# A spectral filter and a PReLU feed-forward block: the first transform's array in another order, its tail in halves, and its first filter load in two parts

## The chip, the cores and the metric

The kernel runs on one core of a Trainium2 chip. The metric is the device time of one execution in microseconds (us). The engines are PE (TensorE: matrix products, with its own weight loads, written PEld), DVE (VectorE), ACT (ScalarE), POOL (GpSimd, which here mostly issues DMAs that convert from float32 to float16), and SP (SyncE, which issues plain DMAs). They run beside each other, each through its own instructions in order, and wait for each other on semaphores. PE writes its results to PSUM, from which ACT or DVE copies them ("evicts" them) to SBUF.

## The reference

```python
X = np.fft.rfft(x, axis=1)                       # x: 8 x 3008 x 256
Y = X * (filt_r + 1j * filt_i)[None, :, :]       # filters: 1505 x 256
y = np.fft.irfft(Y, n=3008, axis=1)
h = y.reshape(24064, 256) @ w_in                 # 256 x 2048
g = np.maximum(h, 0.0) + alpha * np.minimum(h, 0.0)
out = g @ w_out                                  # 2048 x 256
```

So each of the 8 batches is transformed along its 3008 rows, multiplied by one filter, transformed back, and every row then goes through a feed-forward block of width 2048.

## The kernel before

The length 3008 is split as 94 x 32. A transform is a product with a 94-point table, a turn (a transposition), a product with a 32-point table, the filter, the inverse 32-point product, another turn, and the inverse 94-point product. The feed-forward block works on blocks of 512 (one of 384) rows: `Block.up` multiplies by `w_in`, ACT evicts, DVE makes the PReLU, and `Block.down` multiplies by `w_out`. The program is laid out by hand: the text order is the order on each engine.

Seven of the eight transforms are spread in small steps over the feed-forward work of earlier batches (`plan_fft`, `put`), and their turns go through DRAM. The first transform (class `First`, batch 0) has nothing to hide behind. It runs alone at the start, and its turns are products with the identity on PE. Its stages, with the lines of the profile:

- POOL issues the loads of x for batch 0 (L118, eight DMAs), then the filter. `load_filt` (L132-143) issues, for each of the two parts (real, imaginary) and each e in 0, 1, two DMAs of 16 partitions: eight DMAs a call. The calls are for the frequency groups 0 to 4 (L434), 4 to 8 (L455), and 8 to 12, whose real part (L463) and imaginary part (L465) stand on either side of `swapped(8, nc.gpsimd)` (L464), two small POOL operations that make a second inverse table; `swapped(16, nc.gpsimd)` (L468) follows. At group 4 of the loop over groups, POOL issues the loads of `w_in` (L484), of batch 1's x and of `w_out` (L487); a tiny DVE memset of `win_s` (L482) holds the `w_in` loads back until DVE has come that far. Each POOL DMA uses one of eight semaphores in turn, so an issue waits until the DMA issued eight places earlier has landed.
- `piece_a` (L322-336): the 94-point product, eight pieces. The last two pieces are evicted in two parts each, f=0 by ACT and f=1 by DVE, out of one PSUM tile of two banks.
- `turn_at` (L338-345): the first turn, products of `am` with the identity `id16` (L343).
- `piece_b(kp)` for the groups kp = 0 to 11: the 32-point product (L355) and the filter, one DVE product of 128 x 1024 (L360) that reads the filter's group kp.
- `piece_c(kp)`: the inverse 32-point product (L382). Here the filtered data `u` is the stationary operand, the tables `twi_s` and `twx_s` stream; the result goes to PSUM with d on the partitions. `keep_c` evicts it to `vm`, an array of 6144 columns in the order (g, q, k, e), where 4g + e is the row index s and (q, k) the 96 values that the turn puts on partitions.
- `turn` (L393-400): for each s, the 96 columns of `vm` with that s are loaded as the stationary operand. In the order before, neighbours among them are four elements (8 bytes) apart. 64 such products in all (L399): `half_t` makes two values of s, `piece_t` four.
- `half_d` and `pair_d`: the inverse 94-point product (L283) with the table `wi3_s`, whose rows stand in the order (q, k), and the eviction into `yT`, from which the first block starts (`Block.up4`, L569).

After the last group come a fill of three idle products (`warm(3)`, L506, which keep PE busy), `half_t(0)` and `half_t(1)`, evicted by DVE and ACT, two more `half_t` whose eviction comes later, and `half_d(0)` and `half_d(2)`, the two halves of d of the first 376 rows. `up4` multiplies 256 rows by four column groups of `w_in`, both halves kt of d in turn for each group h.

Of the kernel before, what the change touches and what calls it, by code (L numbers as in the profile page):

```python
# [25 lines left out]
def _build_consts():  # L26

    n1, n2, p = np.arange(N1), np.arange(N2), np.arange(32)
    k1 = (2 * (np.arange(NK) // 2) + 24 * (np.arange(NK) % 2))[None, :] + np.arange(2)[:, None]
    k2 = np.where(p < 16, p, 47 - p)  # L30
    g = np.where(p < 16, 1.0, -1.0)

    a1 = 2 * np.pi * n1[:, None, None] * k1[None] / N1
    wf1 = np.stack([np.cos(a1), -np.sin(a1)], axis=2)
    scale = np.where((k1 == 0) | (k1 == 47), 1.0, 2.0)[None, :, None, :] / NFFT
    wi3 = (wf1 * scale).reshape(N1, 96).T
    wfx = wf1.transpose(0, 3, 1, 2).reshape(N1, 96)
# [10 lines left out]
    return wf1, wfx, wfq, wi3, twf  # L48


@with_exitstack
def kernel(
# [8 lines left out]
    out: bass.AP,  # L61
):
    nc = tc.nc
    names = ("wf1", "wfx", "wfq", "wi3", "twf")
# [22 lines left out]
    wfq_s = konst.tile([128, 64], FP16, name="wfq_s")  # L87
    wfx_s = konst.tile([N1, 96], FP16, name="wfx_s")
    wi3_s = konst.tile([96, N1], FP16, name="wi3_s")
    twf_s = konst.tile([128, NK, 64], FP16, name="twf_s")  # L90
    twi_s = konst.tile([128, NK, 64], FP16, name="twi_s")
    filt_s = konst.tile([128, 12, 2, D], FP16, name="filt_s")
# [36 lines left out]
            nc.gpsimd.dma_start(out=hi[32:47], in_=xrow(b, c)[79:94])  # L129
        return lo, hi  # L130

    def load_filt(eng, dst, ha, hb, parts=(0, 1)):  # L132
        n = hb - ha
        for i in parts:
            src = (filt_r, filt_i)[i]
            for e in range(2):
                q = 64 * e + 32 * i
                k = 2 * ha + 24 * e
                for j, step, off in ((0, 1, k), (16, -1, N1 - k)):
                    eng.dma_start(  # L140
                        out=dst[q + j : q + j + 16, ha:hb].rearrange("p h r d -> p (h r) d"),
                        in_=bass.AP(tensor=src.tensor, offset=src.offset + off * D,
                                    ap=[[N1 * D, 16], [step * D, 2 * n], [1, D]]))
# [15 lines left out]
    class Fft:  # L159
        def __init__(self, b):  # L160
            self.b = b
            self.base = (b % 2) * NFFT
            self.uw = {}

        def start_a(self):
# [114 lines left out]
        def inverse(self, pd, g, dh, mh):  # L280
            ps = pd[:, 0 : 4 * N1].rearrange("p (m x) -> p m x", m=4)
            for m in range(4):
                nc.tensor.matmul(ps[:, m], self.zt[:, 8 * g + 4 * mh + m, dh * 128 : dh * 128 + 128],  # L283
                                 wi3_s, start=True, stop=True)
            return ps

        def half_d(self, i, evict, kind, fill=0):
# [19 lines left out]
    def on_dve(o, i):  # L307
        nc.vector.tensor_copy(o, i)  # L308
# [4 lines left out]
    class First(Fft):  # L313
# [7 lines left out]

        def piece_a(self, i, wide):  # L322
            c, sh = i // 2, i % 2
            ps = banks(wide)
            for f in range(2):
                for u in range(4):
                    o = (4 * sh + u) * D + 128 * f
                    nc.tensor.matmul(ps[:, f, 96 * u : 96 * u + 96], xc[(0, c)][0:N1, o : o + 128], wfx_s,
                                     start=True, stop=True)
            o = self.am.rearrange("p (f m s) -> p f m s", f=2, s=N2)[:, :, :, 4 * i : 4 * i + 4]  # L330
            s = ps[:, :, 0:384].rearrange("p f (s m) -> p f m s", s=4)
            if i < 6:
                both[i % 2](o, s)
            else:
                for f in range(2):
                    both[f](o[:, f], s[:, f])

        def turn_at(self, kp, n, evict, wide=False):  # L338
            ps = banks(wide)
# [7 lines left out]
        def piece_b(self, kp):  # L347
            hp = psH.tile([128, 2, 512], FP32, name="hps").rearrange("p r (i d) -> p r i d", i=2)
            for i in range(2):
                for par in range(2):  # L350
                    r = slice(64 * par, 64 * par + 64)
                    for e in range(2):
                        for c in range(2):
                            o = 64 * e + 32 * c
                            nc.tensor.matmul(hp[o : o + 32, par, i],  # L355
                                             twf_s[r, 2 * kp + e, 32 * i : 32 * i + 32],
                                             self.at[kp // 6][r, 2 * kp + e - 12 * (kp // 6)],
                                             start=True, stop=True)
            uu = p_uw.tile([128, 2, 2, D], FP16, name="uu", bufs=3)
            nc.vector.tensor_mul(uu, hp, filt_s[:, kp].unsqueeze(2).to_broadcast([128, 2, 2, D]))  # L360
            self.uw[kp] = uu

        def piece_c(self, kp):
# [7 lines left out]
                self.ops = [t.rearrange("p (k d) -> p k d", k=2) for t in pf]  # L371
            kb = 0 if kp > 9 else kp % 2
            u = self.uw.pop(kp)
            tw, tx = (t.rearrange("p k (c g e) -> p k g c e", c=2, e=4) for t in (twi_s, twx_s))
            for par in range(2):
                for f in range(2):
                    for i, t in enumerate((tw, tx)):
                        for e in range(2):
                            r = slice(64 * e, 64 * e + 64)
                            o = self.ops[e][:, kb].rearrange("p (g w) -> p g w", g=16)  # L380
                            o = o[:, 8 * f : 8 * f + 8, 8 * par : 8 * par + 8]
                            nc.tensor.matmul(o.rearrange("p g (c e) -> p g c e", c=2),  # L382
                                             u[r, par, i, 128 * f : 128 * f + 128], t[r, 2 * kp + par],
                                             start=(i == 0), stop=(i == 1))

        def keep_c(self, kp, evicts, n=2):
            vm = self.vm.rearrange("p (g q k e) -> p g q k e", q=4, k=NK, e=4)
            for e in range(2):
                k = 2 * kp + e
                evicts[e](vm[:, :, :, k : k + 2 * n - 1 : 2],  # L390
                          self.ops[e][:, 0:n].rearrange("p k (g q e) -> p g q k e", q=4, e=4))

        def turn(self, pt, i, n):  # L393
            m = self.vm.rearrange("p (g m e) -> p g m e", m=96, e=4)
            for u in range(n):
                for f in range(2):
                    o = 256 * (u % 2) + 128 * f
                    s = n * i + u
                    nc.tensor.matmul(pt[0:96, u // 2, o : o + 128], m[:, 8 * f + s // 4, :, s % 4], id16,  # L399
                                     start=True, stop=True)  # L400

        def half_t(self, i, kind):
            pt = bank(kind).unsqueeze(1)
# [22 lines left out]
    def swapped(ka, eng):  # L426
        t, o = twi_s[:, ka : ka + 8], twx_s[:, ka : ka + 8]
        eng.tensor_scalar(o[:, :, 32:64], t[:, :, 0:32], gs_s, None, OP.mult)
        eng.tensor_scalar(o[:, :, 0:32], t[:, :, 32:64], gs_s, -1.0, OP.mult, OP.mult)

    xc = {(0, c): load_x(0, c) for c in range(4)}
    f0 = First()
    table(0, 8)
    load_filt(nc.gpsimd, filt_s, 0, 4)  # L434

    def warm(n, pw):
        for _ in range(n):
# [23 lines left out]
    f0.turn_at(2, 2, on_act)  # L461
    inverse_table(8, bank("o"))
    load_filt(nc.gpsimd, filt_s, 8, 12, (0,))  # L463
    swapped(8, nc.gpsimd)  # L464
    load_filt(nc.gpsimd, filt_s, 8, 12, (1,))  # L465
    f0.piece_b(1)
    inverse_table(16, bank("o"))
    swapped(16, nc.gpsimd)  # L468
    f0.piece_b(2)
    f0.turn_at(4, 2, on_act)  # L470
    nc.sync.dma_start(out=wi3_s, in_=consts["wi3"].ap())
# [4 lines left out]
    for r in (slice(0, 64), slice(64, 128)):  # L476
        nc.sync.dma_start(out=wfq_s[r], in_=consts["wfq"].ap()[r])
    for kp in range(12):
        if 0 < kp < 10:
            f0.piece_b(kp + 2)  # L480
        if kp == 4:
            nc.vector.memset(win_s[:, :, 0:1], 0.0)  # L482
            for kt in range(2):
                nc.gpsimd.dma_start(out=win_s[:, kt], in_=moe_w_in[kt * 128 : (kt + 1) * 128])  # L484
# [19 lines left out]
    for o in (32, 96):  # L504
        nc.gpsimd.dma_start(out=filt_s[o : o + 32], in_=filt_s[o - 32 : o])
    warm(3, bank("h"))  # L506
    on_dve(*f0.half_t(0, "o"))
    on_act(*f0.half_t(1, "o"))
    later = [f0.half_t(2, "h"), f0.half_t(3, "f")]
    f0.half_d(0, on_act, "o")  # L510
    f0.half_d(2, on_dve, "o")

    sizes = [512] * 5 + [384] + [512] * 6
    blocks = []
# [21 lines left out]
    class Block:  # L536
# [227 lines left out]
```

## Time and profile before

| what | value |
|---|---|
| median of three runs | 773.95 us (772.74 to 774.29) |
| the profiled execution, its own time | 772.3 us |
| its span, first to last instruction | 770.5 us |
| PE busy | 760.9 us (99%) |
| DVE busy / ACT busy / POOL busy | 634.2 (82%) / 583.2 (76%) / 147.9 us (19%) |
| granted TensorE clock | 1.00 of full speed |

By stretches of the span (busy time of each engine in us, from the view by windows):

| stretch, us | PE | DVE | ACT | POOL | what runs |
|---|---|---|---|---|---|
| 0 to 16.8 | 14.15 | 5.32 | 5.67 | 12.01 | loads, `piece_a`, first turns |
| 16.8 to 30.7 | 12.68 | 13.78 | 11.06 | 12.53 | the twelve groups |
| 30.7 to 34.2 | 3.08 | 1.48 | 2.12 | 0.51 | last group, turn, inverse |
| 34.2 to 47 | 12.04 | 9.80 | 9.58 | 3.60 | first block, more turns |
| 47 to 72 | 24.85 | 22.39 | 20.16 | 2.05 | feed-forward, last turns |
| 72 to 760 | 687.05 | 579.56 | 532.68 | 117.25 | steady work |

"Busy" leaves out waiting and the issue of instructions, except that on POOL the making of a DMA's descriptors is shown as an operation of POOL (DMA_DIRECT2D). A timeline row gives start, length, engine, line, what is written and read, how many instructions are merged, and in brackets how long the engine stood idle before it and what ended that.

### The profile page before, as it was taken

What the parts mean: (1) busy time and instruction counts of PE and PEld (TensorE: products, weight loads), DVE (VectorE), ACT (ScalarE), POOL (GpSimd) and SP (SyncE); (2) the same over time, 40 slices, a digit from 0 to 9 for tenths busy, and PEclk for the clock granted to TensorE, in tenths of its full rate; (3) what the DMA queues carried; (4) which work ended last, traced back from release to release, by engine and by line L of the source; (5) the groups of instructions that cost most, each with busy time, mean ns of one, the idle gap of its engine ahead of it and who ended that gap; (6) DMA issues with size and microseconds to landing.
All of it is one profiled execution on the core that took longest, in us unless ns stands there. A gap on an engine that the chain in (4) does not pass through costs nothing.

```text
span 770.5 us, 16598 instructions
## 1 busy us (share of the span) xinstructions
PE 760.9 (99%) x6550; PEld 510.2 (66%) x6550; DVE 634.2 (82%) x1160; ACT 583.2 (76%) x671; POOL 147.9 (19%) x278
## 2 busy tenths in 40 slices
PE   8999999999999999999999999999999999999998
PEld 4666657666666666666666666766666666766666
DVE  4888885889889998899988998999877888666663
ACT  4787788888778787887778777787767777776663
POOL 7620560132211212121201222022101212000000
PEclk9999999999999999999999999999999999999999
DMA  9995797664954558633883538644473223510111
GB/s 162 148 239 156 134 208 195 171 164 119 200 138 94 138 126 169 185 83 94 188 213 89 124 98 177 182 99 117 119 160 98 68 72 96 152 36 28 42 42 56
DMA packets 96814, 99.77 MB, mean 129 GB/s; under 512 B 12020, under 2 KB 83076, under 8 KB 96544
## 3 DMA queue, kind: packets, MB, share of 16 engines
q1 hardware_dynamic: 82048, 69.22, 32.7%
q0 software_dynamic: 14688, 29.49, 21.4%
q8 instruction: 51, 0.84, 0.5%
q14 instruction: 27, 0.22, 0.1%
HBM read 54.74 MB, written 46.66 MB: 132 GB/s over the span
## 4 chain that ended last, share of the span: by engine, by line
PE 96%; ACT 3%; issue 0%; DVE 0%; DMA 0%; ACTq 0%
PE op L600 42%; PE hps L546 41%; PE psF L283 3%; PE hps L261 2%; PE psF L230 1%; PE hps L176 1%; PE op L438 1%; PE hps L202 1%; ACT asb L305 1%; PE hps L569 1%; ACT v L305 1%; PE op L382 1%; PE psF L399 0%; ACT gtb L577 0%; ACT gtb L555 0%; PE hps L355 0%
## 5 line engine op out<-in xcount | busy, mean ns | idle before, releaser
L555 ACT ACTIVATE gtb<-hps 128x1024 f16<-128x1024 f32 (+1 forms) x376 | 377.4, 1006 | 134.7 <-PE hps L546 131.6
L600 PE MATMUL op<-wout_s,gtb 128*128 128x256 f16 x3008 | 431.4, 273 | 0.0
L546 PE MATMUL hps<-yT,win_s 128*128 128x512 f16 (+1 forms) x1504 | 418.4, 375 | 0.9 <-ACT asb L305 0.5
L600 PEld LDWEIGHTS <-gtb 128*128 128x128 f16 x3008 | 290.8, 98 | 164.5 <-issue 11.0
L558 DVE TENSOR_SCALAR m<-gtb,alm_s 128x512 f16<-128x512 f16 (+1 forms) x752 | 227.2, 346 | 98.4 <-ACT gtb L555 96.9
L560 DVE TENSOR_TENSOR gtb<-gtb,m 128x2048 f16<-128x2048 f16 (+1 forms) x188 | 226.1, 1203 | 10.7 <-DVE m L558 0.5
L546 PEld LDWEIGHTS <-win_s 128*128 128x128 f16 x1504 | 142.5, 98 | 55.2 <-issue 6.6
L244 POOL DMA_DIRECT2D sw<-ww x144 | 71.6, 505 | 414.6 <-DVE ww L237 408.8
L605 ACT ACTIVATE osb<-op 128x512 f32<-128x512 f32 (+1 forms) x97 | 56.6, 584 | 12.6 <-PE op L600 11.5
L305 ACT ACTIVATE asb<-hps 128x1024 f16<-128x1024 f32 (+1 forms) x56 | 56.6, 1020 | 5.6 <-PE hps L176 4.3
L305 ACT ACTIVATE v<-hps 128x1024 f16<-128x1024 f32 (+1 forms) x43 | 43.4, 1010 | 10.8 <-PE hps L261 10.6
L237 DVE TENSOR_TENSOR ww<-psF,filts_s 128x1024 f16<-128x1024 f32 x42 | 51.1, 1218 | 0.2 <-PE psF L230 0.2
L238 DVE TENSOR_TENSOR uu<-psF,filt_s 128x1024 f16<-128x1024 f32 x42 | 51.0, 1214 | 0.0
L305 ACT ACTIVATE yT<-psF 128x752 f16<-128x752 f32 x58 | 46.1, 796 | 2.0 <-PE psF L283 1.9
L283 PEld LDWEIGHTS <-zt 96*128 96x128 f16 x512 | 28.6, 98 | 6.3 <-issue 0.6
L283 PE MATMUL psF<-wi_s,zt 96*128 96x94 f16 x496 | 31.0, 205 | 0.3 <-DVE yT L308 0.2
L249 DVE TENSOR_TENSOR uu<-uu,sw 128x1024 f16<-128x1024 f16 x36 | 24.6, 683 | 1.7 <-DMA sw<-ww 1.3
L242 POOL DMA_DIRECT2D uu<-ww x24 | 19.5, 1238 | 33.0 <-DVE uu L238 24.9
L118 POOL DMA_DIRECT2D xs<-in_x_dram x32 | 21.6, 889 | 13.0 <-PE hps L546 4.9
L186 DVE TENSOR_TENSOR xs<-xs 47x2048 f16<-47x2048 f16 x16 | 19.5, 1220 | 0.4
L190 DVE TENSOR_TENSOR xs<-xs 47x2048 f16<-47x2048 f16 x16 | 19.3, 1209 | 0.0
L261 PE MATMUL hps<-uu,twi_s 64*64 64x256 f16 x336 | 17.3, 281 | 0.0
(86 smaller groups left out, 264.2 us busy)
## 6 DMA issues: line engine op xcount, KB each, us to landing
out_dram<-osb SPq DMA_DIRECT2D x128, 128.0 KB
v_dram<-v SPq DMA_DIRECT2D x84, 128.0 KB
zt<-v_dram SPq DMA_DIRECT2D x28, 384.0 KB
sw<-ww POOLq DMA_DIRECT2D x144, 64.0 KB, 2.8
xs<-in_x_dram POOLq DMA_DIRECT2D x44, 192.0 KB, 6.3
at<-a_dram SPq DMA_DIRECT2D x40, 192.0 KB
a_dram<-asb SPq DMA_DIRECT2D x32, 192.0 KB
a_dram<-asb SPq DMA_DIRECT2D x12, 384.0 KB
```

Source lines behind the costliest of these rows:

```text
L237: nc.vector.tensor_mul(ww, px, fs)
L238: nc.vector.tensor_mul(uu, px, f)
L244: nc.gpsimd.dma_start(out=sw[o : o + 32], in_=ww[i : i + 32])
L261: nc.tensor.matmul(ps[64 * par : 64 * par + 64, e, 256 * h : 256 * h + 256], twi_s[r, 4 * q + 2 * h + par], u[r, par, h], start=True, stop ...
L283: nc.tensor.matmul(ps[:, m], self.zt[:, 8 * g + 4 * mh + m, dh * 128 : dh * 128 + 128], wi3_s, start=True, stop=True)
L305: nc.scalar.activation(o, i, AF.Copy)
L546: nc.tensor.matmul(self.hps[:, j % 2, 0:tn], win_s[:, kt, j * 128 : (j + 1) * 128], yT[:, kt, self.t0 : self.t0 + tn], start=(kt == 0), st ...
L555: nc.scalar.activation(g[:, 2 * i : 2 * i + 2], self.hps[:, :, 0:tn], AF.Copy)
L558: nc.vector.tensor_scalar(m[:, 2 * i + h], g[:, 2 * i + h], 0.0, a, OP.min, OP.mult)
L560: nc.vector.tensor_add(g, g, m)
L600: nc.tensor.matmul(self.op[:, si - s0], self.gts[k][:, 128 * si : 128 * si + 128], wout_s[:, k], start=(si == s0 and k == 0), stop=(si == ...
L605: nc.scalar.activation(osb[:, 0:m], self.op[:, 0:m], AF.Copy)
```

## The change

- `keep_c` writes, and `turn` reads, `vm` in the order (s, k, q): the 96 columns of one s are now contiguous. `piece_c` writes PSUM in the order (s, q) to match, reads its tables with c innermost, and runs f outermost, so that a half of d is finished before the other. The first transform's inverse uses its own table `wif_s`, with its rows in the new order (`self.wi`).
- In group 11 the filter's product, and both evictions in `keep_c`, are made in two halves of d.
- The first four values of s are turned by `side_t(0)` (first half of d, evicted by ACT) and `side_t(1)` (second half, by DVE), in place of `half_t(0)` and `half_t(1)`. `half_d(0)` is now evicted by DVE and `half_d(2)` by ACT.
- The filter's groups 0 to 4 are loaded by two calls, 0 to 2 and 2 to 4, each of eight DMAs of half the size. `swapped(8)` is split into its two operations, with two filter DMAs between them. The loads from L484 on stand at group 3 and not 4.
- The last two pieces of `piece_a` take a PSUM tile for each f: piece 6 two of the `o` kind (which the idle products use too), piece 7 two of the `h` kind.
- `up4` runs kt outermost: four products with the first half of d, then four with the second.
- SP loads `wif`, and `wi3` later; `wfq` in one DMA in place of two.

```diff
@@ class Fft / First
+            self.wi = wi3_s if b else wif_s
 def piece_a(self, i, wide):
-            ps = banks(wide)
+            if i < 6:
+                ps = banks(wide)
+                pf = [ps[:, f] for f in range(2)]
+            else:
+                pf = [bank("oh"[i - 6]) for f in range(2)]
...
 def piece_b(self, kp):
-            nc.vector.tensor_mul(uu, hp, filt_s[:, kp].unsqueeze(2).to_broadcast([128, 2, 2, D]))
+            for d in ((slice(0, 128), slice(128, D)) if kp == 11 else (slice(0, D),)):
+                w = 128 if kp == 11 else D
+                nc.vector.tensor_mul(uu[:, :, :, d], hp[:, :, :, d],
+                                     filt_s[:, kp, :, d].unsqueeze(2).to_broadcast([128, 2, 2, w]))
 def piece_c(self, kp):
-            tw, tx = (t.rearrange("p k (c g e) -> p k g c e", c=2, e=4) for t in (twi_s, twx_s))
-            for par in range(2):
-                for f in range(2):
+            tw, tx = (t.rearrange("p k (c s) -> p k s c", c=2) for t in (twi_s, twx_s))
+            for f in range(2):
+                for par in range(2):
...
-                            o = self.ops[e][:, kb].rearrange("p (g w) -> p g w", g=16)
-                            o = o[:, 8 * f : 8 * f + 8, 8 * par : 8 * par + 8]
-                            nc.tensor.matmul(o.rearrange("p g (c e) -> p g c e", c=2),
+                            o = self.ops[e][:, kb].rearrange("p (s q) -> p s q", q=4)
+                            nc.tensor.matmul(o[:, 32 * f : 32 * f + 32, 2 * par : 2 * par + 2],
 def keep_c(self, kp, evicts, n=2):
+            vm = self.vm.rearrange("p (s k q) -> p s k q", q=4, k=NK)
+            for s in ((slice(0, 32), slice(32, 64)) if kp == 11 else (slice(0, 64),)):
+                for e in range(2):
+                    k = 2 * kp + e
+                    evicts[e](vm[:, s, k : k + 2 * n - 1 : 2],
+                              self.ops[e][:, 0:n].rearrange("p k (s q) -> p s k q", q=4)[:, s])
 def turn(self, pt, i, n):
-            m = self.vm.rearrange("p (g m e) -> p g m e", m=96, e=4)
+            m = self.vm.rearrange("p (f s m) -> p f s m", f=2, m=96)
...
+        def side_t(self, f):
+            pt = bank("o")
+            for u in range(4):
+                nc.tensor.matmul(pt[0:96, 128 * u : 128 * u + 128],
+                                 self.vm.rearrange("p (f s m) -> p f s m", f=2, m=96)[:, f, u], id16,
+                                 start=True, stop=True)
+            return self.zt[:, 0:4, 128 * f : 128 * f + 128], pt[0:96].rearrange("p (s d) -> p s d", s=4)
@@ the order by hand
-    load_filt(nc.gpsimd, filt_s, 0, 4)
+    load_filt(nc.gpsimd, filt_s, 0, 2)
+    load_filt(nc.gpsimd, filt_s, 2, 4)
...
-    swapped(8, nc.gpsimd)
-    load_filt(nc.gpsimd, filt_s, 8, 12, (1,))
+    swapped(8, nc.gpsimd, (0,))
+    load_filt(nc.gpsimd, filt_s, 8, 12, (1,), (0,))
+    swapped(8, nc.gpsimd, (1,))
+    load_filt(nc.gpsimd, filt_s, 8, 12, (1,), (1,))
...
-        if kp == 4:
+        if kp == 3:
             nc.vector.memset(win_s[:, :, 0:1], 0.0)
...
-    on_dve(*f0.half_t(0, "o"))
-    on_act(*f0.half_t(1, "o"))
+    on_act(*f0.side_t(0))
+    on_dve(*f0.side_t(1))
     later = [f0.half_t(2, "h"), f0.half_t(3, "f")]
-    f0.half_d(0, on_act, "o")
-    f0.half_d(2, on_dve, "o")
+    f0.half_d(0, on_dve, "o")
+    f0.half_d(2, on_act, "o")
@@ def up4
-            for h in range(4):
-                j = 4 * i + h
-                for kt in range(2):
+            for kt in range(2):
+                for h in range(4):
+                    j = 4 * i + h
                     nc.tensor.matmul(ps[:, h], win_s[:, kt, j * 128 : (j + 1) * 128], yT[:, kt, t],
-                                     start=(kt == 0), stop=(kt == 1))
+                                     start=(kt == 0 and h % 2 == 0), stop=(kt == 1 and h % 2 == 1))
```

More of the change, by code (lines that the diff above doesn't have):

```diff
@@ L36, in _build_consts @@
     wi3 = (wf1 * scale).reshape(N1, 96).T
+    wif = (wf1 * scale).transpose(3, 1, 2, 0).reshape(96, N1)
     wfx = wf1.transpose(0, 3, 1, 2).reshape(N1, 96)
@@ L47, in _build_consts @@
     twf = fwd.transpose(3, 0, 2, 4, 1, 5).reshape(128, NK, 64)
-    return wf1, wfx, wfq, wi3, twf
+    return wf1, wfx, wfq, wi3, wif, twf
 @with_exitstack
@@ L63 @@
     nc = tc.nc
-    names = ("wf1", "wfx", "wfq", "wi3", "twf")
+    names = ("wf1", "wfx", "wfq", "wi3", "wif", "twf")
     consts = {n: nc.inline_tensor(np.ascontiguousarray(v).astype(np.float16), name="c_" + n)
@@ L89 @@
     wi3_s = konst.tile([96, N1], FP16, name="wi3_s")
+    wif_s = konst.tile([96, N1], FP16, name="wif_s")
     twf_s = konst.tile([128, NK, 64], FP16, name="twf_s")
@@ L130, in load_halves, with load_filt @@
         return lo, hi
-    def load_filt(eng, dst, ha, hb, parts=(0, 1)):
+    def load_filt(eng, dst, ha, hb, parts=(0, 1), es=(0, 1)):
         n = hb - ha
@@ L135, in load_filt @@
             src = (filt_r, filt_i)[i]
-            for e in range(2):
+            for e in es:
                 q = 64 * e + 32 * i
@@ L283, in inverse @@
                 nc.tensor.matmul(ps[:, m], self.zt[:, 8 * g + 4 * mh + m, dh * 128 : dh * 128 + 128],
-                                 wi3_s, start=True, stop=True)
+                                 self.wi, start=True, stop=True)
             return ps
@@ L327, in piece_a @@
                     o = (4 * sh + u) * D + 128 * f
-                    nc.tensor.matmul(ps[:, f, 96 * u : 96 * u + 96], xc[(0, c)][0:N1, o : o + 128], wfx_s,
+                    nc.tensor.matmul(pf[f][:, 96 * u : 96 * u + 96], xc[(0, c)][0:N1, o : o + 128], wfx_s,
                                      start=True, stop=True)
             o = self.am.rearrange("p (f m s) -> p f m s", f=2, s=N2)[:, :, :, 4 * i : 4 * i + 4]
-            s = ps[:, :, 0:384].rearrange("p f (s m) -> p f m s", s=4)
             if i < 6:
-                both[i % 2](o, s)
+                both[i % 2](o, ps[:, :, 0:384].rearrange("p f (s m) -> p f m s", s=4))
             else:
                 for f in range(2):
-                    both[f](o[:, f], s[:, f])
+                    both[f](o[:, f], pf[f][:, 0:384].rearrange("p (s m) -> p m s", s=4))
         def turn_at(self, kp, n, evict, wide=False):
@@ L386, in keep_c @@
         def keep_c(self, kp, evicts, n=2):
[L387 to L391, printed above, removed]
+            vm = self.vm.rearrange("p (s k q) -> p s k q", q=4, k=NK)
[4 more added lines that the diff above has]
+                              self.ops[e][:, 0:n].rearrange("p k (s q) -> p s k q", q=4)[:, s])
         def turn(self, pt, i, n):
-            m = self.vm.rearrange("p (g m e) -> p g m e", m=96, e=4)
+            m = self.vm.rearrange("p (f s m) -> p f s m", f=2, m=96)
             for u in range(n):
@@ L397, in turn @@
                     o = 256 * (u % 2) + 128 * f
[L398 to L399 removed]
+                    nc.tensor.matmul(pt[0:96, u // 2, o : o + 128], m[:, f, n * i + u], id16,
                                      start=True, stop=True)
+        def side_t(self, f):
[5 more added lines that the diff above has]
+            return self.zt[:, 0:4, 128 * f : 128 * f + 128], pt[0:96].rearrange("p (s d) -> p s d", s=4)
         def half_t(self, i, kind):
@@ L424, in inverse_table, with swapped @@
         on_act(twi_s[:, ka : ka + 8].rearrange("p k m -> p (k m)"), pb)
-    def swapped(ka, eng):
+    def swapped(ka, eng, parts=(0, 1)):
         t, o = twi_s[:, ka : ka + 8], twx_s[:, ka : ka + 8]
-        eng.tensor_scalar(o[:, :, 32:64], t[:, :, 0:32], gs_s, None, OP.mult)
-        eng.tensor_scalar(o[:, :, 0:32], t[:, :, 32:64], gs_s, -1.0, OP.mult, OP.mult)
+        if 0 in parts:
+            eng.tensor_scalar(o[:, :, 32:64], t[:, :, 0:32], gs_s, None, OP.mult)
+        if 1 in parts:
+            eng.tensor_scalar(o[:, :, 0:32], t[:, :, 32:64], gs_s, -1.0, OP.mult, OP.mult)
     xc = {(0, c): load_x(0, c) for c in range(4)}
@@ L470 @@
     f0.turn_at(4, 2, on_act)
-    nc.sync.dma_start(out=wi3_s, in_=consts["wi3"].ap())
+    nc.sync.dma_start(out=wif_s, in_=consts["wif"].ap())
     nc.sync.dma_start(out=al16, in_=moe_alpha.rearrange("(j p) -> j p", p=128))
@@ L475 @@
         nc.sync.dma_start(out=wf1_s[r], in_=consts["wf1"].ap()[r])
-    for r in (slice(0, 64), slice(64, 128)):
-        nc.sync.dma_start(out=wfq_s[r], in_=consts["wfq"].ap()[r])
+    nc.sync.dma_start(out=wfq_s, in_=consts["wfq"].ap())
+    nc.sync.dma_start(out=wi3_s, in_=consts["wi3"].ap())
     for kp in range(12):
```

## The prediction

> **What bounds the kernel now.** The page first. PE is busy 99% of the span, and the chain that ended last is 96% PE, so from about 47 us on a microsecond is won only by giving PE less to do. Before that the profile has to be read by stage, because the first transform runs alone. The timeline of DVE shows what sets that stage:
>
> ```profile
> 16.84 9.16 DVE L360 TENSOR_TENSOR uu<-hps,filt_s 128x1024 f16<-128x1024 f32 x8 [0.49 <-DMA filt_s<-in_filt_r_dram]
> 24.81 0.06 DVE L482 MEMSET win_s<- 128x2 f16 x1
> 25.91 4.76 DVE L360 TENSOR_TENSOR uu<-hps,filt_s 128x1024 f16<-128x1024 f32 x4
> ```
>
> The twelve filter products run back to back, one every 1.13 us, from 16.84 to 30.68. The first waited 0.49 us for the filter; no other waited for it. So the stage ends when DVE does, as long as each group's filter is there in time. Whether it is, POOL's timeline tells:
>
> ```profile
> 12.72 0.53 POOL L140 DMA_DIRECT2D filt_s<-in_filt_i_dram  x1 [0.46 <-DMA xs<-in_x_dram]
> 13.25 2.01 POOL L140 DMA_DIRECT2D filt_s<-in_filt_r_dram  x4
> 15.25 1.49 POOL L140 DMA_DIRECT2D filt_s<-in_filt_i_dram  x3
> 17.00 0.53 POOL L140 DMA_DIRECT2D filt_s<-in_filt_i_dram  x1 [0.26 <-DMA filt_s<-in_filt_i_dram]
> 17.53 2.01 POOL L140 DMA_DIRECT2D filt_s<-in_filt_r_dram  x4
> 19.67 0.94 POOL L428 TENSOR_SCALAR gtb<-twi_s,signs_s 128x256 f16<-128x256 f16 x1
> 20.58 0.48 POOL L429 TENSOR_SCALAR gtb<-twi_s,signs_s 128x256 f16<-128x256 f16 x1
> 21.01 2.12 POOL L140 DMA_DIRECT2D filt_s<-in_filt_i_dram  x4
> 23.16 0.95 POOL L428 TENSOR_SCALAR gtb<-twi_s,signs_s 128x256 f16<-128x256 f16 x1
> 24.09 0.48 POOL L429 TENSOR_SCALAR gtb<-twi_s,signs_s 128x256 f16<-128x256 f16 x1
> 25.18 1.14 POOL L484 DMA_DIRECT2D win_s<-in_moe_w_in_dram  x2 [0.61 <-DVE win_s L482]
> ```
>
> An issue costs POOL about 0.5 us (0.484 to 0.569 over the 24 of L140), and from 13.25 to 24.57 POOL is full but for some 0.4 us. The view of `filt_s`, narrowed to the last issue of each third, gives 4.0, 3.3 and 2.5 us from issue to landing, so the thirds are complete at 16.72, 20.29 and 25.09. Groups 4 and 8 began on DVE at 21.38 and 25.92: a margin of 1.1 and 0.8 us.
>
> Last, the groups by form on PE's weight loads (busy us, mean ns of one):
>
> ```profile
> L399 PEld LDWEIGHTS <-v 128*96 128x96 f16 x64 | 6.5, 182 | 0.7 <-ACT v L305 0.4
> L176 PEld LDWEIGHTS <-wf_s 94*96 94x96 f16 x48 | 5.5, 124 | 0.8 <-issue 0.5
> L343 PEld LDWEIGHTS <-gtb 128*128 128x128 f16 x48 | 2.8, 97 | 1.2 <-DVE gtb L308 0.5 <-issue 0.4
> L230 PEld LDWEIGHTS <-twf_s 64*64 64x64 f16 x336 | 8.7, 106 | 3.0 <-issue 3.0
> L355 PEld LDWEIGHTS <-twf_s 64*32 64x32 f16 x192 | 1.8, 89 | 2.2 <-issue 0.8 <-DVE uu L360 0.7
> ```
>
> The second turn (L399) loads 96 columns spaced by four elements; in the instruction starts its products follow each other every 90 ns. The first turn (L343), with the same 128 streamed columns and contiguous weights, does so every 56 ns.
>
> **Part 1: the filter's first third in two calls.** Eight more POOL issues. Half-size DMAs save few descriptors; the nearest rows for the price per descriptor are `w_in` (0.57 us) and `w_out` (0.92 us, some 900 more), 0.4 ns each, so I take 0.49 us an issue, 3.9 us in all. POOL is then at: groups 2 to 4 issued by 17.1, 4 to 8 by 21.1, the real part of 8 to 12 by 23.1, first half of `swapped(8)` (0.13 + 0.94) 24.2, two issues 25.25, second half (0.48 as L429, or 0.94 as L428, which also follows a DMA) 25.75 to 26.2, two issues 26.8 to 27.25. The last four DMAs before landed 1.95 us after their issue ended; groups 8 to 12 are there at 28.75 to 29.2, DVE takes group 8 at about 29.1.
>
> What it gives: groups 0 and 1 can start at about 16.35 and not 16.84, since their filter lands 1 to 1.5 us earlier and the last `piece_a` is evicted by both engines at once (before, DVE waited 0.52 us for ACT on the same tile). But `warm(5)` now waits for an `o` bank, so the turn itself gains only some 0.2 us. All of it is lost again at group 2 (there at 19.1 to 20.1; 19.12 before) and group 4 (23.1 to 23.9, 21.38 before), and the end is set by group 8: 29.1 against 25.92, **+3.2 us** (2.9 to 3.5). The second half of `swapped(8)`, which `piece_c(4)` waits for, ends at 26.2 at the latest, when the fifth product has run; PE catches up before 29.1. Moving the `w_in` loads to group 3 buys nothing, as POOL and no longer DVE holds them: they are issued at 28.2 to 28.7 and by their 5.3 and 8.3 us land by 37.5.
>
> Group 11 before waited 0.15 us for PE; after a stall PE is ahead, so that goes. Two half products cost one more start, 0.07 us. The stage ends at 33.75 against 30.68: **+3.1 us** (2.85 to 3.4).
>
> **Part 2: the tail in halves.** Before, from the end of the last product to the last of the first eight products of L569: 30.68 to 35.2, 4.5 us. After, from T = 33.75: the second half of `piece_c(11)` and both evictions end at T+1.0 (four of 128 columns at about 0.27 each, from 0.38 for 256; the same-bank products come first in the text, so the eviction's first half doesn't overlap them), side_t(0) at T+0.85 behind the three fills, ACT's eviction (0.59) to T+1.9, DVE's (0.69) to T+2.3, inverse, `yT` by DVE (0.55) to T+2.9 and by ACT (0.48) to T+3.25. The first half of d starts `up4` at T+2.95, the second follows at T+3.4 or when `w_in` is there, at most T+3.7; the eight end at T+3.85 to 4.1. **-0.6 us** (-0.75 to -0.2). If the eviction of one half waited for the other, it would be the small end.
>
> **Part 3: contiguous columns.** 64 products at 90 ns. What does a contiguous load of 96 columns allow? L355, L230 and L176 take 89, 106 and 124 ns for 32, 64 and 96 columns: 0.55 ns a column on 71 fixed; alone, a strided one takes 163 (the least of L399), which less 71 is 92, its spacing. So contiguous ones could follow every 53 ns, and the 128 streamed columns set 56: 34 ns saved, 64 times 2.2 us; the other bound is nothing. The first 16 are in the tail above. Of the other 48 (1.6 us), 32 fall in the stretch 47 to 72, where PE is busy 24.85 of 25.0 us: -1.1. The 16 between 35 and 39 save 0.54, of which I count half, since ACT ends several waits of that stage. **-1.35 us** (-1.6 to 0).
>
> **Part 4: what `piece_c` reads and writes.** Its tables now stream with neighbours 64 bytes apart, and it writes PSUM in runs of two. No row streams so; L382 makes a pair in 29 ns, full speed for 64 columns. Between that and the factor of 2.2 that the strided weights show (1.2 against 0.55 ns a column) lies 0 to 0.28 us a piece. PE waits in most of the stage, so only the last pieces count: **+0.1 us** (0 to 0.5). Nothing for the rest: SP's DMAs are over by 17.4 and first needed at 36; the larger number of `keep_c` instructions is in part 2; `neg` and the loads behind POOL's delay have 3 us and more of margin (`w_out` landed at 40.8, used at 45.8, and both move).
>
> **Sum.** +3.1 - 0.6 - 1.35 + 0.1 = +1.25 us. The profiled execution would go from 772.3 to 773.55. Its own time lies 1.65 below the median shown, so the change is put on the median: 773.95 + 1.25 = **775.2 us**, its own range 774.3 to 776.5.
>
> **Rival A: the issues cost nothing that lasts.** If the eight more issues overlapped with what POOL waits for anyway, DVE would run through from 16.35 and end at 30.25: -0.4, then -0.6 and -1.4 of parts 2 and 3: -2.4, 771.55 us. For it: POOL waited 3.7 us for x before 12.7. Against: those waits lie ahead of the added issues, and no issue among 24 was under 0.48 us. The Trainium skill, "DMA: Bandwidth & Descriptors", section "Anatomy of one DMA — SWDGE (gpsimd) path", has some 50 ns of dispatch and a small descriptor cost; eight such would add about 0.4 us, an estimate, and give this rival. POOL's row, 0.5 us each without a gap, speaks against that. 18%.
>
> **Rival B: the turns stay bound by their weights.** All loads under 100 ns back to back are 128 wide; the turn loads 96. If the width and not the step is what costs, 90 ns remain: part 3 is gone (+1.35), and 0.3 of part 2: +2.9, 776.85 us. It decides from 34 us on. For it: no contiguous 96 wide load runs back to back here. Against: L176's 124 ns against 163. The Trainium skill, "TensorE: Matmul & The Clock Gate", section "LDWEIGHTS (loading the stationary operand)", gives columns over 1.2 in ns, 80 for 96; that would leave a saving of 10 ns a product, 0.6 us. The slope of 0.55 ns over three rows here is less steep. 17%.
>
> **Rival C: the streamed tables are slow.** Part 4 at its upper bound, POOL at the late end of its bracket, part 2 at -0.2 since the last group is then late on PE too, and half of part 3 hidden behind DVE: 3.4 + 0.5 - 0.2 - 0.7 = +3.0, 776.95 us. Against it: PE has time to spare up to group 11. 6%.
>
> **Rival D: half of the delay**, if the small DMAs land in less than 1.95 us and DVE's lead is partly kept: about 773.9 us. 9%.
>
> **How the numbers follow.** The forecast has 50%. A measurement of this kernel tells 0.2% (1.55 us) from no change, so the bounds are 772.4 and 775.5. Faster: A, 0.18. Slower: B, C and the upper 0.36 of the forecast, 0.41. Within: the rest, 0.41. The range takes in half of A and nearly all of B: 771.8 to 777.3.
>
> **What would show it.** Right: POOL's issues of L140 end near 27, DVE idles before groups 4 and 8 for `filt_s`, group 11 ends near 33.8, weight loads of the second turn near 124 ns with products every 56. Wrong: twelve products without a gap (A); 90 ns between the turns' products (B); pairs of `piece_c` at more than 29 ns (C). A wait of `up4` for `win_s` beyond 0.5 us would add to the sum.

## The result, and the profile after

The changed kernel takes 776.12 us (median of six runs, 775.33 to 776.84) against 772.73 us for the kernel before on the same chip: a ratio of 1.0039 with a 95% interval of 1.0026 to 1.0052, so 3.0 us slower (2.0 to 4.0). The forecast was slower by 1.25 us, in a range that holds the measured time. From run to run the time tends to go with the granted clock: the three runs with a mean clock of 0.998 took 775.33 to 776.27 us, the three with 0.993 to 0.996 took 775.96 to 776.84, and the profiled one (775.38) is of the first kind. The span of the profiled execution went from 770.5 to 773.6 us, its granted clock from 1.00 to 0.998 on average.

The timeline of DVE in the changed kernel (start, length, engine, line, what it writes and reads, number merged, idle time before it and what ended that):

```profile
16.36 2.36 DVE L368 TENSOR_TENSOR uu<-hps,filt_s 128x1024 f16<-128x1024 f32 x2 [0.40 <-DMA filt_s<-in_filt_r_dram]
19.02 2.35 DVE L368 TENSOR_TENSOR uu<-hps,filt_s 128x1024 f16<-128x1024 f32 x2 [0.30 <-DMA filt_s<-in_filt_i_dram]
23.93 3.50 DVE L368 TENSOR_TENSOR uu<-hps,filt_s 128x1024 f16<-128x1024 f32 x3 [2.55 <-DMA filt_s<-in_filt_r_dram]
...
29.41 3.48 DVE L368 TENSOR_TENSOR uu<-hps,filt_s 128x1024 f16<-128x1024 f32 x3 [0.86 <-DMA filt_s<-in_filt_i_dram]
33.49 1.29 DVE L368 TENSOR_TENSOR uu<-hps,filt_s 128x512 f16<-128x512 f32 x2 [0.59 <-PE hps L361]
```

The unbroken row of twelve products now has four holes. The first pair starts 0.48 us earlier, the time that the prediction gave; that the two-part load is the reason isn't shown, as kernels with the load in one call start at 16.48 to 17.34 (e3, e11). Groups 2, 4 and 8 wait for the filter, group 8 until 29.41 us (25.91 before), and group 11 waits for PE. POOL's timeline shows why the filter is late:

```profile
13.17 1.98 POOL L142 DMA_DIRECT2D filt_s<-in_filt_r_dram  x4
15.13 1.98 POOL L142 DMA_DIRECT2D filt_s<-in_filt_i_dram  x4
17.10 2.06 POOL L142 DMA_DIRECT2D filt_s<-in_filt_r_dram  x4
19.11 2.06 POOL L142 DMA_DIRECT2D filt_s<-in_filt_i_dram  x4
21.12 2.08 POOL L142 DMA_DIRECT2D filt_s<-in_filt_r_dram  x4
23.25 1.01 POOL L445 TENSOR_SCALAR gtb<-twi_s,signs_s 128x256 f16<-128x256 f16 x1
24.14 1.17 POOL L142 DMA_DIRECT2D filt_s<-in_filt_i_dram  x2
25.27 0.55 POOL L447 TENSOR_SCALAR gtb<-twi_s,signs_s 128x256 f16<-128x256 f16 x1
25.70 1.11 POOL L142 DMA_DIRECT2D filt_s<-in_filt_i_dram  x2
```

POOL is full from 13.17 on. The last filter issue ends at 26.81, where before it ended at 23.14. The weight loads of the second turn, by form (busy us, mean ns of one):

```profile
L407 PEld LDWEIGHTS <-v 128*96 128x96 f16 x56 | 3.9, 123 | 0.5
```

They fell from 182 to 123 ns, and in the instruction starts the turn's products follow each other every 56 ns (89 before). Two things the prediction had priced at next to nothing are in the same trace. The first is the inverse product `piece_c`, in PE's timeline of the kernel before (L382) and of the changed one (L390):

```profile
22.15 0.19 PE L382 MATMUL op<-gtb,uu 64*128 64x64 f16 x2
22.18 0.19 PE L382 MATMUL op<-twi_s,uu 64*128 64x64 f16 x2
```

```profile
21.71 0.26 PE L390 MATMUL op<-twi_s,uu 64*128 64x64 f16 x2
21.77 0.26 PE L390 MATMUL op<-gtb,uu 64*128 64x64 f16 x2
```

A pair of products starts every 29 ns before and every 62 ns after (medians over the pieces). The second is the granted clock, in the view by windows of the changed kernel (length, then busy time of PE, PEld, DVE, ACT and POOL with instructions in brackets, granted clock, DMA share, GB/s):

```profile
24.00:25.00 1.00, 0.00 (x0) 0.00 (x0) 1.00 (x1) 1.00 (x2) 1.00 (x3) 1.00 0.64 77
...
27.00:28.00 1.00, 1.00 (x21) 0.90 (x16) 1.00 (x2) 0.54 (x2) 1.00 (x2) 0.55 0.76 106
28.00:29.00 1.00, 1.00 (x24) 0.39 (x24) 0.56 (x1) 1.00 (x3) 1.00 (x3) 0.50 0.19 21
29.00:30.00 1.00, 1.00 (x32) 0.52 (x30) 0.59 (x1) 0.46 (x1) 1.00 (x3) 0.50 0.96 66
```

PE stood idle for 1.55 us ahead of group 6's product, which waited for DVE and so for the filter. Some 2 us after it had gone back to work its clock fell to 0.50, for about 3.4 us (27.1 to 30.5).

Followed along the same instructions in both traces, the delay grows and shrinks so:

| point | before | after | later by |
|---|---|---|---|
| group 8's filter product starts | 25.91 | 29.41 | 3.50 |
| group 11's product starts | 29.45 | 33.49 | 4.04 |
| last of the first eight L569 (L590) starts | 35.09 | 39.17 | 4.09 |
| first `down` product | 45.76 | 49.51 | 3.75 |
| the 300th `up` product | 199.52 | 202.82 | 3.30 |

From there to the last `up` product (3.27) the two traces run nearly in parallel; at the end of the span 3.1 us are left.

### The profile page after: what moved, and what is told of

The parts are those of the page before. It is cut to its first block, busy times and chain, and to the rows that moved or that the text cites. A ratio compares the mean times of both kernels' runs of the same rounds, so it can differ in the third digit from the quotient of the medians.

```text
span 773.6 us, 16614 instructions
## 1 busy us (share of the span) xinstructions
PE 762.4 (99%) x6550; PEld 510.9 (66%) x6550; DVE 633.8 (82%) x1162; ACT 583.1 (75%) x672; POOL 151.7 (20%) x286
## 4 chain that ended last, share of the span: by engine, by line
PE 92%; DVE 2%; POOL 2%; ACT 2%; DMA 1%; issue 0%; ACTq 0%; POOLq 0%
PE op L621 42%; PE hps L567 41%; PE psF L286 3%; PE hps L264 2%; POOL filt_s L142 1%; PE psF L233 1%; DMA xs<-in_x_dram 1%; PE hps L179 1%; PE hps L205 1%; DVE gtb L604 1%; DVE zt L311 1%; ACT asb L308 1%; DVE m L603 1%; PE op L390 0%; POOL xs L120 0%
## 5 line engine op out<-in xcount | busy, mean ns | idle before, releaser
L286 PE MATMUL psF<-wi_s,zt 96*128 96x94 f16 x448 | 27.9, 205 | 0.1
L368 DVE TENSOR_TENSOR uu<-hps,filt_s 128x1024 f16<-128x1024 f32 (+1 forms) x13 | 14.1, 1137 | 4.7 <-DMA filt_s<-in_filt_r_dram 3.0
```

## The experiments

All runs are compared with runs of the kernel before on the same chip (medians 772.87 to 772.91 us).

**e1: the load in one call again, all else as changed.**

```diff
-    load_filt(nc.gpsimd, filt_s, 0, 2)
-    load_filt(nc.gpsimd, filt_s, 2, 4)
+    load_filt(nc.gpsimd, filt_s, 0, 4)
```

> The changed kernel with the filter's groups 0 to 4 loaded by one call again; all else as changed. Theory 1 (POOL's eight added issues of 0.5 us set the stage's end): the filter's thirds are complete near 16.7, 20.3 and 25.1 us again, DVE's twelve products run without a gap of over 0.5 us, group 8 starts near 26 and not at 29.41, the granted clock stays at 1.00 (no idle of PE of 1.5 us), and the time falls by 3.5 us (3.0 to 4.4) against the changed kernel, to about 772.5 us. Theory 2 (the pairs of piece_c at 62 ns, double those of before, set the stage's end): with twelve pieces that take 0.25 us longer each, group 11 still ends past 33 us and the time falls by 1 us at most. Rival A of the prediction (the issues cost nothing): no change.

Measured: 774.35 us, ratio 1.0012 (1.0003 to 1.0021). It falls by 1.8 us against the changed kernel's median, half of what theory 1 gave and more than theory 2's 1 us. DVE's timeline of e1:

```profile
20.38 1.23 DVE L368 TENSOR_TENSOR uu<-hps,filt_s 128x1024 f16<-128x1024 f32 x1 [0.15 <-PE hps L361]
21.87 2.49 DVE L368 TENSOR_TENSOR uu<-hps,filt_s 128x1024 f16<-128x1024 f32 x2 [0.27 <-DMA filt_s<-in_filt_r_dram]
...
24.63 2.49 DVE L368 TENSOR_TENSOR uu<-hps,filt_s 128x1024 f16<-128x1024 f32 x2 [0.25 <-PE hps L361]
27.39 3.62 DVE L368 TENSOR_TENSOR uu<-hps,filt_s 128x1024 f16<-128x1024 f32 x3 [0.27 <-PE hps L361]
31.96 1.29 DVE L368 TENSOR_TENSOR uu<-hps,filt_s 128x512 f16<-128x512 f32 x2 [0.94 <-PE hps L361]
```

All these holes are PE's. The view puts the one before 21.87 down to a DMA, but the filter of groups 4 to 8 had landed by 20.82, and group 4's `piece_b` ended at 21.80. `piece_b` comes late by a loop that the chain of waits (start, length, what) shows:

```profile
20.31 0.64 PE op L390 x16
20.95 1.08 ACT v L308 x2
...
22.07 0.65 PE op L390 x15
22.73 0.34 PE hps L361 x16
```

Two pieces of `piece_c`, one `piece_b` between them, and ACT's eviction of both pieces, for which the next one waits, make 2.76 us for two groups; DVE needs 2.27. Group 11 starts 2.5 us later than before. The clock stayed at 1.00. So both theories hold in part: behind the late filter stood a second limit.

**e2: `piece_c` streams contiguous runs; the load stays in two parts.**

```diff
-            tw, tx = (t.rearrange("p k (c s) -> p k s c", c=2) for t in (twi_s, twx_s))
+            tw, tx = (t.rearrange("p k (c s) -> p k c s", c=2) for t in (twi_s, twx_s))
...
-                            o = self.ops[e][:, kb].rearrange("p (s q) -> p s q", q=4)
-                            nc.tensor.matmul(o[:, 32 * f : 32 * f + 32, 2 * par : 2 * par + 2],
+                            o = self.ops[e][:, kb].rearrange("p (q s) -> p q s", q=4)
+                            nc.tensor.matmul(o[:, 2 * par : 2 * par + 2, 32 * f : 32 * f + 32],
...
-                              self.ops[e][:, 0:n].rearrange("p k (s q) -> p s k q", q=4)[:, s])
+                              self.ops[e][:, 0:n].rearrange("p k (q s) -> p s k q", q=4)[:, s])
```

> The changed kernel with piece_c's tables streamed in contiguous runs of 32, the product written to PSUM in the order (q, s), and the reordering left to keep_c's read; the two-part filter load stays. The pairs of piece_c follow each other every 29 ns again. Theory 1: group 8's filter still lands near 29.3, so only the last groups and the tail gain: 0.5 us less than the changed kernel (0.2 to 1.0). Theory 2: the time falls by 2.5 us or more.

Measured: 775.65 us, ratio 1.0030 (1.0019 to 1.0041), 0.5 below the changed kernel in the medians, though the two were compared on different chips and the intervals overlap. The pairs are at 29 ns, but 53 ns in the pieces that fall where the clock is 0.50. As theory 1 said: with the filter late, faster streams buy little. The row of e2 from group 8 on has no hole left:

```profile
30.39 4.68 DVE L368 TENSOR_TENSOR uu<-hps,filt_s 128x1024 f16<-128x1024 f32 x5 [1.66 <-DMA filt_s<-in_filt_i_dram]
```

But group 8 starts at 30.39 and not near 29.3, because here the last filter DMA landed only at 30.26 (29.29 in the changed kernel). So its stage ends no earlier.

**e3: e1 and e2 together.**

> One call for the filter's first third and contiguous streams in piece_c together; the contiguous turns and the tail in halves stay. If both causes are the ones named: the stage ends at about 30.3 to 30.7, the turns still follow every 56 ns, and the time is 1.5 us (0.7 to 2.3) below the kernel before, about 771.3 us, so 4.5 below the changed one. If the contiguous turns and the halves are worth nothing here, it equals the kernel before.

Measured: 771.72 us, ratio 0.9983 (0.9972 to 0.9995), 4.4 below the changed kernel and faster than the one before. DVE's timeline of e3:

```profile
16.48 8.20 DVE L368 TENSOR_TENSOR uu<-hps,filt_s 128x1024 f16<-128x1024 f32 x7 [0.21 <-PE hps L361]
...
24.59 4.61 DVE L368 TENSOR_TENSOR uu<-hps,filt_s 128x1024 f16<-128x1024 f32 x4
29.36 1.29 DVE L368 TENSOR_TENSOR uu<-hps,filt_s 128x512 f16<-128x512 f32 x2 [0.16 <-PE hps L361]
```

The row has no hole over 0.3 us again. The two repairs alone bring 1.8 and 0.5 us, together 4.4: the stage ends with the later of two limits, so removing one shows only the other. In the traces group 11 ends at 34.78 in the changed kernel, 33.25 in e1, 35.07 in e2 and 30.65 in e3 (30.68 before). Priced the other way, on top of good streams the two-part load costs 3.9 us (775.65 - 771.72), and on top of the one-part load the streams cost 2.6 (774.35 - 771.72).

**e4: the kernel before with its first load in two parts, nothing else.**

> The kernel before with its one call for groups 0 to 4 made into two, and nothing else. Theory 1: group 8 starts on DVE near 29.2 and not at 25.92, the stage ends 3 us later, and the time rises by 3.2 us (2.7 to 4.0); PE idles over a microsecond before group 6's product and its granted clock may fall for a few us. Theory 2 and rival A: at most 0.5 us slower.

Measured: 776.14 us, ratio 1.0038 (1.0025 to 1.0051), 3.3 us slower. DVE's timeline of e4:

```profile
24.18 4.63 DVE L360 TENSOR_TENSOR uu<-hps,filt_s 128x1024 f16<-128x1024 f32 x4 [2.71 <-DMA filt_s<-in_filt_r_dram]
...
30.15 4.62 DVE L360 TENSOR_TENSOR uu<-hps,filt_s 128x1024 f16<-128x1024 f32 x4 [1.34 <-PE hps L355]
```

Two lines of the diff make as much of a slowdown as the whole change. Group 8 starts 1 us later than expected. The view puts its wait down to PE, which was at a clock of 0.50 from 27.0 to 30.4 us, but PE had made group 8's product by 29.02:

```profile
28.39 0.63 PE L355 MATMUL hps<-at,twf_s 64*32 64x256 f16 x16
```

The last filter DMA was issued at 27.18, after POOL had waited 0.76 us for another landing, and landed at 30.02. Group 8 waits for the filter here too.

**e5 and e6: which half of the changed access is slow, the streamed read or the PSUM write?** One run each. e5 reads contiguous runs and writes single elements four apart; e6 reads as the changed kernel and writes contiguous runs of 64 (with `keep_c` reading accordingly). The core of the edits:

```diff
# e5, against the changed kernel
-            tw, tx = (t.rearrange("p k (c s) -> p k s c", c=2) for t in (twi_s, twx_s))
+            tw, tx = (t.rearrange("p k (c s) -> p k c s", c=2) for t in (twi_s, twx_s))
-                            o = self.ops[e][:, kb].rearrange("p (s q) -> p s q", q=4)
+                            o = self.ops[e][:, kb].rearrange("p (s q) -> p q s", q=4)
# e6, against the changed kernel
-                            o = self.ops[e][:, kb].rearrange("p (s q) -> p s q", q=4)
+                            o = self.ops[e][:, kb].rearrange("p (r s c) -> p r s c", r=2, c=2)
```

> The changed kernel with piece_c's tables streamed in contiguous runs of 32, but the product written to PSUM as single elements four apart. If the streamed read (neighbours 64 bytes apart) is what makes a pair take 62 ns, the pairs are back at 29 ns here; if it is the PSUM write, they stay at 62 ns or more. The time is 0.5 us below the changed kernel in the first case, the same in the second.

> The counterpart: the tables streamed as in the changed kernel (neighbours 64 bytes apart), and the product written to PSUM in contiguous runs of 64. If the streamed read is the cause, the pairs stay at 62 ns; if the write is, they are at 29 ns. The time is that of the changed kernel in the first case.

PE's timeline of e5, then of e6:

```profile
19.88 0.25 PE L390 MATMUL op<-twi_s,uu 64*128 64x64 f16 x2
19.93 0.25 PE L390 MATMUL op<-gtb,uu 64*128 64x64 f16 x2
```

```profile
19.50 0.27 PE L390 MATMUL op<-gtb,uu 64*128 64x64 f16 x2
19.56 0.26 PE L390 MATMUL op<-twi_s,uu 64*128 64x64 f16 x2
```

e6: 62 ns with a contiguous write, so the streamed read alone explains the changed kernel's pairs. e5 was not the clean counterpart it was meant to be: writing single elements four apart costs nearly as much by itself, 53 to 56 ns. The two costs are of different kinds: in the stretch at a clock of 0.50 e6's pairs, and the changed kernel's, still take 62 ns, and e5's take 106. What the changed kernel's runs of two would cost with a contiguous read was not tried. Both kernels have the two-part load and take the changed kernel's time within the scatter of single runs (775.74 and 776.47 us).

**e7: e4 with seven idle products in the place where PE waited.**

```diff
+        if kp == 4:
+            warm(7, bank("o"))
         if 0 < kp < 10:
             f0.piece_b(kp + 2)
```

> The kernel before with the filter's first third in two calls, as e4, and seven idle products of 512 columns ahead of group 6's product, where PE waited 2.6 us. Theory 3 (PE's idle time lets the granted clock fall to 0.50 for some 3.4 us, and that is a second price of the late filter): the clock stays at 1.00 from 26 to 31 us, group 8 starts near 29.3 when its filter lands, and not at 30.15, and the time is 0.9 us (0.5 to 1.2) below e4, about 775.2 us. If the clock costs nothing beside the filter's delay, the time is that of e4.

Measured: 775.63 us, ratio 1.0042 (1.0030 to 1.0055). The clock stays at 1.00 from 22 to 33 us, all pieces at 29 ns, so PE's idle time is what let the clock fall in e4. But against e4's 1.0038 the time doesn't differ. In the traces group 8 starts at 29.57 and not 30.15, and the delay at the 300th `up` is 3.52 against 4.11 us; that isn't the clock's price either, because the last filter DMA landed at 29.45 here and at 30.02 in e4, and from group 8's start both kernels need 4.62 us to the end of group 11. The drop of the clock is real, and no price of it shows here; theory 3's second half failed.

**e8: e3 without the halves** (group 11 whole, `half_t(0)` and `half_t(1)` in place of `side_t`, `half_d` evicted as before).

```diff
-            for d in ((slice(0, 128), slice(128, D)) if kp == 11 else (slice(0, D),)):
+            for d in (slice(0, D),):
...
-    on_act(*f0.side_t(0))
-    on_dve(*f0.side_t(1))
+    on_dve(*f0.half_t(0, "o"))
+    on_act(*f0.half_t(1, "o"))
```

> e3 (one load, contiguous streams, contiguous turns) without the halves: group 11's product and its evictions whole, half_t(0) and half_t(1) in place of side_t, half_d evicted as before; up4 keeps its order. The prediction gave the halves about 0.6 us less some 0.3 for the faster turns in that stretch: the time rises by 0.4 us (0.1 to 0.7) against e3, to about 772.1 us. If the halves are worth nothing, no change.

Measured: 771.63 us, ratio 0.9989 (0.9977 to 1.0001), e3's time. In the traces the stretch from group 11 to the eighth L569 shortens by 0.60 us in e3 and by 0.41 in e8, so the halves are worth about 0.2 us there. That is inconclusive as a time.

**e9: the kernel before with eight tiny POOL DMAs behind the first filter load.**

```diff
     load_filt(nc.gpsimd, filt_s, 0, 4)
+    tiny = konst.tile([128, 8, 16], FP16, name="tiny")
+    for i in range(8):
+        nc.gpsimd.dma_start(out=tiny[0:16, i], in_=filt_r[16 * i : 16 * i + 16, 0:16])
```

> The kernel before with eight small POOL DMAs of 16 rows x 64 bytes, into a tile that nothing reads, behind the load of the filter's groups 0 to 4; every filter DMA has the size it had. Theory 1 (what costs is POOL's time per issue, in series with the later filter loads): group 2 is not late, group 4 starts near 24 and group 8 near 29 to 30 on DVE, as in e4, and the time rises by 3.2 us (2.5 to 4.2). Theory 4 (what costs is that DMAs of half the size land less well): at most 0.7 us slower, since these carry next to nothing.

Measured: 777.03 us, ratio 1.0057 (1.0043 to 1.0070), 4.1 us slower. POOL's timeline of e9:

```profile
13.46 3.34 POOL L437 DMA_DIRECT2D tiny<-in_filt_r_dram  x7
17.50 0.48 POOL L437 DMA_DIRECT2D tiny<-in_filt_r_dram  x1 [0.70 <-DMA filt_s<-in_filt_i_dram]
```

DMAs that carry next to nothing take POOL 0.48 us each and cost as much as the two-part load, with every filter DMA at its full size. Size is excluded; it is the issues, and the waits for a landing that come with them (0.70 us before the eighth here). Group 2 was not late, and groups 4 and 8 started at 24.86 and 30.69, later than expected. In the trace the excess over e4 lies in the last filter DMA, which landed at 30.57 against 30.02 us.

**e10: the first load in three calls**, so 16 issues more than before.

```diff
-    load_filt(nc.gpsimd, filt_s, 0, 4)
+    for a, b in ((0, 2), (2, 3), (3, 4)):
+        load_filt(nc.gpsimd, filt_s, a, b)
```

> The kernel before with the filter's groups 0 to 4 loaded by three calls (0 to 2, 2 to 3, 3 to 4), so 16 more issues than before and 8 more than e4. Theory 1: POOL is 7.9 us later, groups 8 to 12 land near 33 us, and the time rises by 7 us (6 to 9) over the kernel before, twice that of e4 or a little more. If only the first delay counts and the rest is hidden, about 4 us.

Measured: 779.90 us, ratio 1.0093 (1.0079 to 1.0107), 7.0 us slower. Eight issues cost 3.3 us, sixteen 7.0: 0.41 to 0.44 us an issue, close to the 0.5 us that one takes on POOL. Group 8's filter landed at 33.32.

**e11: the contiguous array alone, on the kernel before** (`vm` in the order (s, k, q) with its own inverse table, `piece_c` as in e2, `keep_c` reordering on its read). The core, against the kernel before:

```diff
-            m = self.vm.rearrange("p (g m e) -> p g m e", m=96, e=4)
+            m = self.vm.rearrange("p (f s m) -> p f s m", f=2, m=96)
...
-            tw, tx = (t.rearrange("p k (c g e) -> p k g c e", c=2, e=4) for t in (twi_s, twx_s))
+            tw, tx = (t.rearrange("p k (c s) -> p k c s", c=2) for t in (twi_s, twx_s))
```

> The kernel before with the contiguous array alone: vm in the order (s, k, q), its own inverse table, piece_c's tables streamed in contiguous runs with f outermost, keep_c reordering on its read; the loads, the tail, piece_a and up4 as before. Turns every 56 ns. From the shifts in e8: 0.9 us below the kernel before (0.4 to 1.4), about 771.9 us, the same as e8 within 0.4. If piece_a's separate tiles or up4's order bring some of e8's gain, this one gains less than 0.4.

Measured: 771.68 us, ratio 0.9983 (0.9974 to 0.9992), 1.3 us faster than the kernel before (0.6 to 2.0) and level with e3 and e8. It is the simplest of the kernels that beat the one before and the changed one. Its trace gives 0.4 us at the 300th `up`, but its first product started 0.50 us later than in the kernel before (17.34 against 16.84: its first filter third landed at 17.22 and not 16.72), so the gain from group 8 on is 0.9.

## Why the prediction was right in its way and short in its size

**Part 1 (the load in two calls, +3.1 us at the stage's end): right as far as group 8.** POOL's issues ended at 26.81 (26.8 to 27.25 foreseen) and group 8 started at 29.41 (29.1); the last DMA landed 2.5 us after its issue had ended, and not 1.95 as before. In every kernel whose last filter DMA came late, group 8 starts about 0.12 us after that DMA has landed (landings from the traces' semaphore records; e5 and e6 do the same):

| kernel | last filter DMA lands | group 8 starts | group 11 ends | from group 8's start to that end |
|---|---|---|---|---|
| changed | 29.29 | 29.41 | 34.78 | 5.37 |
| e2 | 30.26 | 30.39 | 35.07 | 4.68 |
| e4 | 30.02 | 30.15 | 34.77 | 4.62 |
| e7 | 29.45 | 29.57 | 34.19 | 4.62 |
| e9 | 30.57 | 30.69 | 35.30 | 4.61 |
| e10 | 33.32 | 33.44 | 38.06 | 4.62 |

e4 measures the part alone at +3.3 us, e9 and e10 show that it is the number of issues. Rival D, half of the delay, is out: in e4 and e7 the stage ends 4.1 and 3.5 us later. Rival A is out, and with it the Trainium skill's "DMA: Bandwidth & Descriptors", section "Anatomy of one DMA — SWDGE (gpsimd) path", as a price for POOL: 50 ns of dispatch and a small cost of descriptors, against the 0.48 us that each of e9's tiny ones takes.

**Part 4 (what `piece_c` streams, +0.1 us): here a step failed.** The factor itself stood in the text as the upper bound, 2.2, and came true (62 against 29 ns). What was wrong is "PE waits in most of the stage, so only the last pieces count", and with it part 1's "PE catches up before 29.1" and "after a stall PE is ahead". The pieces after the stall count. The changed kernel's chain of waits (start, length, what) doesn't go through group 8's filter but along PE:

```profile
25.27 0.56 POOL gtb L447
...
25.87 0.61 PE op L390 x14
...
30.11 0.65 PE op L390 x16
30.76 1.08 ACT v L308 x2
...
31.89 0.65 PE op L390 x15
32.54 0.54 PE psF L457 x2
33.07 0.34 PE hps L361 x16
```

PE works without a gap until 30.76, then must wait for ACT's eviction, and `piece_b` for group 11 comes 0.59 us late. From group 8's start the stage needs 5.37 us, and with contiguous streams 4.61 to 4.68. Two things delayed PE, each by about 0.9 us, an estimate from the rows: four pieces took 0.45 us each and not 0.22, and at a clock of 0.50 a turn took 1.03 us and not 0.62, two `piece_b` 0.63 and not 0.41 each. e1 shows that slow streams at a clock of 1.00 hold up the stage by themselves, and e2, e4, e9 and e10, where the clock fell too, that with contiguous streams the fall costs nothing from group 8 on; but there group 8 started later than in the changed kernel, so how the 0.7 us divide is open. The stage ended 4.1 us later, not 3.1: 0.3 from the landing and 0.7 from PE.

**Part 2 (the tail, -0.6 us): the sum's term did not appear in the changed kernel** (delay 4.04 at group 11, 4.09 at the eighth L569), because PE was still behind: it came to the slow product of group 10 only at 34.61 us, as DVE was about to end group 11 (34.78). The late filter isn't the reason: over the same stretch e2, with the late filter and contiguous streams, gains 0.61 us (4.34 to 3.73), e3 0.60, and e1, with the early filter and slow streams, nothing (2.50 to 2.56). So the streams cost this term as well. Of the 0.60, e8 keeps 0.41 without the halves, and e11, with the contiguous array alone, 0.20; the rest of e8's is from what else it keeps of the change, the order of `up4` among it, which no run has alone.

**Part 3 (contiguous columns, -1.35 us): right in kind, too large.** 123 ns a load and 56 ns a product are the numbers foreseen, so rival B, that the width of 96 sets the pace, is out. The delay fell from 4.09 to 3.30 us, 0.8 and not 1.35; in e1, e2, e3, e8 and e11 it falls by 0.75 to 0.78 from the same product on. The first two of the four later turns lie where the changed kernel's chain runs through DVE and not PE:

```profile
52.71 1.23 DVE gtb L604
53.94 1.06 DVE m L603 x4
...
55.02 1.22 DVE gtb L604
56.25 0.53 DVE m L579 x2
56.77 1.13 DVE zt L311
```

These lines of the chain of waits (start, length, what) have DVE back to back; PE's saving there is given back: the delay of the `up` products goes from 3.75 to 3.27 us behind these two turns, and is 3.74 again before the last two. The prediction halved the gain only before 47 us, where 0.34 came of 0.27 foreseen, and took it whole after, where 0.45 came of 1.1. In e11, by time, the part is worth 1.3 us.

So +3.1 became +4.1 at the end of the stage, -0.6 became 0, and -1.35 became -0.8: 3.3 us in the trace, for 1.25 foreseen. This is nearest to rival C, by its mechanism (the slow streams) as by its +3.0 us, which was given 6%; but rival C took the streams for 0.5 us at the stage's end, and left 0.2 of part 2.

That 776.12 us lies inside the forecast's own range, 774.3 to 776.5, is luck. That range was put on a median of 773.95 us for the kernel before, and stands for 0.35 to 2.55 us slower; the kernel before then measured 772.73 in six runs, and the change costs 3.0 us (3.4 in the medians).

## What to carry to other kernels

A DMA issued from POOL has a price on POOL whatever it carries; cutting a load in two to have its head earlier moves every later load behind it, so look for the margin of the last one first. When two limits lie close together, undo them together as well as one by one: 1.8 and 0.5 us apart were 4.4 us in one. A new order of an array is a choice for everyone who touches it: here the reordering cost nothing where ACT reads PSUM (0.60 us an eviction of `piece_c` in e11 as before), and most where PE streams.

## What the runs showed of the hardware that was not expected

- PE's granted clock fell to 0.50 for about 3.4 us after an idle of 1.55 us, and it fell some 2 us after PE had gone back to work. In e6 an idle of 1.51 us and in e4 one of 2.62 us were followed by the same; seven products in its place (e7) prevented it, and e7's later idle of 1.32 us was not followed by a fall. In e10, with idles of 2.74 and 2.19 us, the clock stayed at 0.50 for 10.24 us. The Trainium skill, "TensorE: Matmul & The Clock Gate", section "Why this matters for your kernels", asks for no gaps over some 3 us; 1.51 us was enough here.
- Streamed columns whose neighbours lie 64 bytes apart halve PE's rate: 62 against 29 ns a pair of 64 columns. The 62 ns don't change at a clock of 0.50, where contiguous pairs go from 29 to 53 ns, so here it isn't PE's clock that sets the pace. The Trainium skill, "Advanced Engine Details and Errata", section "Memory Cachelines", has lines of 16 bytes in SBUF, a penalty for a new line at each access, and two hits on a line as enough. The streamed read agrees. The turn's weight loads don't: at 8 bytes apart they hit each line twice, and still took 182 ns against 123.
- Single elements written four apart into PSUM cost nearly as much, 53 to 56 ns a pair (e5), with a contiguous read; at a clock of 0.50 it is 106 ns.
- A wait that a view puts down to the engine that signalled last can be another's: in e4 group 8's is put down to PE, and in e1 group 4's to a DMA, and what was needed of either had been there for 1 us.
